# Attention block with gated MLP on one core: the last head set fed to the out-projection in padded layout, own MLP buffers for the last two chunks, and head loads on one queue

## The chip, the cores and the metric

The kernel runs on one core of a Trainium2 chip, as one launch. The metric is the device time in microseconds (us), the median over several executions. Lower is better. One further execution was recorded by the hardware profiler; all readings of single instructions, waits and stretches come from that record, which spans 899.9 us.

## The reference, cut to what matters

S = 2048 rows, D = 640, 32 heads of 20 columns, F = 1536, all bf16. The condition vector `c` gives six modulation vectors of 640 (shift, scale and gate for each half).

```python
mod = (silu(c) @ w_mod).reshape(1, 6, 1, 640)
sa, ca, ga, sb, cb, gb = mod[:, 0], ..., mod[:, 5]

h = layernorm(x) * (1 + ca) + sa
q, k, v = split_heads(h @ wqkv)                 # 32 heads of 20
p = softmax(q @ k.T * 20 ** -0.5)               # 32 x 2048 x 2048 scores
x = x + ga * (merge_heads(p @ v) @ wo)

h = layernorm(x) * (1 + cb) + sb
x = x + gb * (((h @ w_gate) * (h @ w_up)) @ w_down)
```

## The kernel before

The Python of the kernel does not emit its instructions in the order in which it is written. It builds tasks with dependencies, priorities and estimated durations, runs a small list scheduler over them at build time, and emits for each engine the order that came out, with semaphore waits in between. On the chip that order is fixed. Constants such as `QUADS`, `FILL_MIN` or `DMA_RATE` therefore change the order of instructions, or how many of a kind there are; nothing of them is read at run time.

The work is cut in five query chunks, and each chunk in eight head sets of four heads. Heads stand at a pitch of 32 partitions, so that four heads use the four row groups (scores) or the four column groups (attention times V) of TensorE at once.

```python
CHUNKS = [(0, 512), (512, 512), (1024, 512), (1536, 256), (1792, 256)]   # (first row, rows)
QUADS = [2, (2, 3, 3, 3, 3, 3, 3, 3), (2, 3, 3, 3, 3, 3, 3, 3), 1, 1]    # per chunk, or per head set
NPS = 8
D_RES = 8
FILL_MIN = 3400.0
LATEQ = ()
```

One unit of scores is 128 keys x 512 (or two times 128 keys x 256) of one head: one PSUM bank. Most units are turned to exponentials by ScalarE (ACT), three and two units in turn per instruction (groups of banks A and B). A "quad" is four units that VectorE (DVE) handles instead: it forms a 16-bit integer whose bits, read as bf16, approximate the exponential, and adds five shifted copies of it, all of which are multiplied with V:

```python
        def fexp(e, nu=nu, b0=b0, cellp=cellp):                       # ACT, 3 or 2 units
            return e.activation(PP[:, cellp["p"], 0:nu * 512],
                                ps[:, b0:b0 + nu, :].rearrange("p b c -> p (b c)"), AFT.Exp, scale=ESCALE)
...
            def fp1(e, st_=st_, x=x, cell=cell):                      # DVE, 4 per quad
                return e.tensor_scalar(DB0[:, st_["slot"], x * 512:(x + 1) * 512], bank(cell["b"]), EBIAS, 0.0,
                                       op0=ALU.add, op1=ALU.max)
...
            def fsh(e, st_=st_, cell=cell, jj=jj):                    # DVE, 5 per quad
                return e.tensor_scalar(DSS[:, cell["s"], :], DB0[:, st_["slot"], :], float(SHIFTS[jj]), None, op0=ALU.add)
```

The first loads go out on two queues, in this order of code (the last string but one is the issuing engine, the number its priority):

```python
    d_c = dma("act", 1280, ...)
    load_x(0, 0, "sp", 0);      load_x(0, 1, "act", 0.5)       # rows 0-255, 256-511
    load_wm(0, wm_a[0], "sp", 1);  load_wm(1, wm_a[1], "act", 1)   # modulation: shift, scale
    load_w(d_wk, 0, ..., "sp", 2); load_w(d_wq, 0, ..., "act", 2)  # half of Wk, of Wq
    load_x(1, 0, "sp", 1.5);    load_x(1, 1, "act", 1.5)
    ...
```

In chunk 0 the kernel also normalizes all rows, transposes them and projects K, V and Q; Q of the row blocks 1 to 3 stands at the end of that list. When a head set is done, DVE transposes the sum, divides by the softmax denominator (row 0 of each head's 32) and transposes back into `OcT`. There the heads lie at a pitch of 32 partitions; small DMAs move their 20 rows each into `Ocp`, where all 640 rows are dense in five blocks of 128:

```python
        t4 = dve(n * 1.1 + 65, lambda e: e.transpose(OcT[:, cell["s"], 0:n], OTn[:, 0:n]), [t3], prio=1.5)
        pcs = oc_pieces(j)                       # 4 or 5 pieces per head set
        ...
                return e.dma_start(Ocp[r0:r0 + nr, slot, b5, 0:n],
                                   OcT[32 * s + 1 + ro:32 * s + 1 + ro + nr, cell["s"], 0:n])
```

When the chunk's eight sets are in `Ocp`, `suffix(ci)` runs for it: out-projection, residual, second layernorm, gate and up projections, product, down-projection, store. For all but the last chunk these rounds are spread among the next chunk's attention, by gates that count exponential groups. All chunks share one set of buffers (`hprod`, `h2T`, `xck`, `xn2`):

```python
        d_xc = dma("sp", ..., lambda e: e.dma_start(xck[:, 0:ntl, :], xv[:, t0:t0 + ntl, :]),
                   out_prev + proj_early, prio=15, gate=max(0, gb - 20))    # residual rows
        for tl in range(ntl):
            for hf in range(2):
                for k in range(KD):                                          # KD = 5
                    f = quarters(320, lambda k=k, tl=tl: Ocp[:, slot, k, tl * 128:(tl + 1) * 128],
                                 lambda k=k, hf=hf: wo_sb[:, k, 320 * hf:320 * hf + 320], k == 0, k == KD - 1)
                ...
                r = Round(mms, list(oc_ready[ci]) + t_wo + [d_xc], after, pr(), gate=gate(KD * 320), name=f"op{ci}.{tl}")
```

`out_prev` are the stores of the chunk before, `proj_early` all projections. The gates `ga` and `gb` are multiplied into `wo` and `wd` (the down-projection weights) once, by GpSimd (POOL), after those weights are loaded; `wd` is loaded when the last projection has run, as its place was theirs. TensorE's idle time is filled with matmuls on the identity when the recent activity falls under `FILL_MIN`, to keep its clock up.

Of the kernel before, what the change touches and what calls it, by code (L numbers as in the profile page):

```python
# [18 lines left out]
DMA_RATE_2 = 180.0  # L19
DMA_SHARED = 12000.0  # L20
HAM_W = 3413.3
# [72 lines left out]
class Sched:  # L94
# [67 lines left out]
    def finish_issue(self, task, start, dur):  # L162
        task.start = start
        if task.nbytes:
            b = max(self.dma_free.get(task.eng, 0.0), start + dur)
            self.dma_free[task.eng] = b + task.nbytes / (DMA_RATE_2 if b < DMA_SHARED else DMA_RATE)
            task.done = self.dma_free[task.eng] + 1400.0
# [187 lines left out]
QUADS = [2, (2, 3, 3, 3, 3, 3, 3, 3), (2, 3, 3, 3, 3, 3, 3, 3), 1, 1]  # L355
# [3 lines left out]
NPS = 8  # L359
D_LATE = 12  # L360
D_RES = 8
PVMIN, PVMAX, PVCAP = 10, 10, 16
GATE_F = [0.7, 0.7, 0.6, 0.5, 1.0]
FILL_MIN = 3400.0
# [3 lines left out]
LN2P = 0.7  # L368
HT_L = 0.12
# [4 lines left out]
LATEQ = ()  # L374
LATEQ_A = 2
# [13 lines left out]
def build_kernel(nc, A_x, A_wqkv, A_wo, B_x, B_w_gate, B_w_up, B_w_down, c, w_mod, out):  # L389
# [97 lines left out]

    PP = alloc("PP", [128, NPS, 3 * 512], BF16)

# [43 lines left out]
    NSX = 11  # L533
    q_dead = sum(NSET * n * 2 for (_, n) in CHUNKS[:-1])
    nsx = min(NSX, q_dead // (2 * KD * 128 * 2))
    stx = [at("stx", [128, 2, KD, 128], BF16, qt_off + i * 2 * KD * 128 * 2) for i in range(nsx)]
# [5 lines left out]
    pP = Slots(list(range(NPS)), "PP")  # L542
# [29 lines left out]
    d_c = dma("act", 1280, lambda e: e.dma_start(c5[:, :], cv[:, :]), prio=0, dur=550.0)  # L572
# [19 lines left out]
    load_x(0, 0, "sp", 0)  # L592
    load_x(0, 1, "act", 0.5)
    load_wm(0, wm_a[0], "sp", 1)
    load_wm(1, wm_a[1], "act", 1)
    load_w(d_wk, 0, 1, wk_sb, 0, "sp", 2)
    load_w(d_wq, 0, 0, wq_sb, 0, "act", 2)
    load_x(1, 0, "sp", 1.5)
    load_x(1, 1, "act", 1.5)
# [157 lines left out]
    proj_early = []  # L757

# [4 lines left out]
    def kq_round(kind, j, tc, prio, gate=0):  # L763
# [33 lines left out]
        if kind == "K" or tc not in LATEQ:  # L797
            proj_early.append(r.last)

    def v_round(t, ch, prio, gate=0):  # L800
# [19 lines left out]
        proj_early.append(r.last)  # L820
# [128 lines left out]
    d_wo = dma("sp", 128 * KD * D * 2, lambda e: e.dma_start(wo_sb[:], wov[:, :, :]), prio=10)  # L949
    t_wo = []  # L950
    for k in range(KD):
        t_wo.append(pool(1400, lambda e, k=k: e.tensor_tensor(wo_sb[:, k, :], wo_sb[:, k, :], gab[:, 0, :], ALU.mult),
                         [d_wo] + ev_ga, prio=20))
# [30 lines left out]
    for g, (us, b0) in enumerate(glist):  # L984
# [14 lines left out]
        def fexp(e, nu=nu, b0=b0, cellp=cellp):  # L999
            return e.activation(PP[:, cellp["p"], 0:nu * 512],  # L1000
                                ps[:, b0:b0 + nu, :].rearrange("p b c -> p (b c)"), AFT.Exp, scale=ESCALE)
        if nu:
            ta = Task("act", nu * 512 / 1.2 + 52.0, fexp, [ts], prio=g, name=f"E{g}")
            ta.acq = [(pP, "p", nu)]

            def on_e(task, g=g, us=us, bset=bset, cellp=cellp):
# [3 lines left out]
                for i, u in enumerate(us):  # L1010
                    u.pslot = (pP, PP, task.slots["p"])
# [68 lines left out]

    oc_ready = {}
    oc_free = {}

    def item_end_tasks(it):
# [14 lines left out]
        pcs = oc_pieces(j)  # L1099
        t4.acq = [(sOcT, "s", len(pcs))]  # L1100
# [6 lines left out]
        for (b5, s, r0, nr, ro) in pcs:  # L1107
# [3 lines left out]
            dps = [t4]  # L1111
# [7 lines left out]
        oc_ready.setdefault(ci, []).extend(dms)  # L1119
        sc.left += 1  # L1120
# [3 lines left out]
    sfx_done = {}  # L1124
    sStg = [Slots(list(range(NSTG)), "stg") for _ in range(2)]
    out_prev = []

    def suffix(ci):
        nonlocal out_prev
# [17 lines left out]
        def pr():  # L1147
            return pbase + rc_[0]
# [519 lines left out]
```

The softmax here doesn't subtract the row's maximum and nothing guards it: scores larger than these inputs give would overflow.

## Time and profile before

| what | value |
|---|---|
| median of 3 executions | 897.82 us (897.0 to 901.93) |
| profiled execution | 899.9 us, mean granted TensorE clock 0.977 |
| exponentials on ACT | 695 instructions, 793.8 us, first at 23.2 us, last ends at 856.7 us |
| quads: first step, shifted copies (DVE) | 312 x 681 ns, 390 x 695 ns |
| copies into `Ocp` | 180 DMAs |

How to read it: a share of busy time is an average over the whole span. The stages differ: a head in which loads and projections come first, the long middle with its exponentials, and a tail that only the last chunk's MLP fills. So the views that follow are cut by stage. In a group's line stand the source line, the engine, the operation, what it writes and reads, how often it ran; then its busy time, the mean of one in ns, and the idle time of the engine before it with what ended it.

### The profile page before, as it was taken

What the parts mean: (1) busy time and instruction counts of PE and PEld (TensorE: products, weight loads), DVE (VectorE), ACT (ScalarE), POOL (GpSimd) and SP (SyncE); (2) the same over time, 40 slices, a digit from 0 to 9 for tenths busy, and PEclk for the clock granted to TensorE, in tenths of its full rate; (3) what the DMA queues carried; (4) which work ended last, traced back from release to release, by engine and by line L of the source; (5) the groups of instructions that cost most, each with busy time, mean ns of one, the idle gap of its engine ahead of it and who ended that gap; (6) DMA issues with size and microseconds to landing.
All of it is one profiled execution on the core that took longest, in us unless ns stands there. A gap on an engine that the chain in (4) does not pass through costs nothing.

```text
span 899.9 us, 31137 instructions
## 1 busy us (share of the span) xinstructions
PE 851.7 (95%) x13944; PEld 338.3 (38%) x13944; DVE 727.2 (81%) x1330; ACT 801.4 (89%) x712; POOL 56.8 (6%) x89
## 2 busy tenths in 40 slices
PE   6899999999999899999998999999999999999968
PEld 3434333333322222223333333333344445545547
DVE  6978677777868999899878999998888777688743
ACT  1567999999999789999999999999999999999901
POOL 4203000000000710000001000000010000000000
PEclk7989999999999889999999999999999999999999
DMA  9320000000006002210220011100301326405210
GB/s 307 103 75 7 5 6 5 2 6 6 5 5 166 2 20 50 50 34 6 49 64 5 23 44 42 42 6 20 74 27 28 70 65 129 95 28 109 51 32 18
DMA packets 100550, 42.31 MB, mean 47 GB/s; under 512 B 81218, under 2 KB 100418, under 8 KB 100418
## 3 DMA queue, kind: packets, MB, share of 16 engines
q1 hardware_dynamic: 98552, 38.44, 17.1%
q8 instruction: 110, 1.80, 0.8%
q10 hardware_dynamic: 1866, 1.89, 0.7%
q14 instruction: 22, 0.18, 0.1%
HBM read 35.06 MB, written 2.62 MB: 42 GB/s over the span
## 4 chain that ended last, share of the span: by engine, by line
PE 49%; ACT 32%; DVE 12%; issue 4%; POOL 1%; DMA 1%; SPq 0%; ACTq 0%; POOLq 0%; DVEq 0%
ACT PP L1000 32%; PE ps_all L653 15%; PE ps_all L969 14%; PE ps_all L1362 13%; PE ps_all L768 5%; DVE DSS L1038 2%; DVE DB L1024 2%; DVE xn L1180 1%; DMA x<-in_A_x_dram 1%; DVE st L711 1%; DVE st L1173 1%; DVE xck L1164 1%; POOL rs L1178 1%; DVE hT L746 1%; DVE xn L720 0%
## 5 line engine op out<-in xcount | busy, mean ns | idle before, releaser
L1000 ACT ACTIVATE PP<-ps_all 128x1536 bf16<-128x1536 f32 (+1 forms) x695 | 793.8, 1278 | 46.1 <-PE ps_all L969 42.3
L969 PE MATMUL ps_all<-QT,KT 32*128 32x512 bf16 (+1 forms) x2623 | 292.3, 343 | 14.5 <-ACT PP L1000 8.8
L1038 DVE TENSOR_SCALAR DSS<-DB 128x2048 int16<-128x2048 int16 x390 | 264.8, 695 | 29.5 <-PE ps_all L1362 27.1
L1024 DVE TENSOR_SCALAR DB<-ps_all 128x512 int16<-128x512 f32 x312 | 211.4, 681 | 42.8 <-PE ps_all L969 41.4
L969 PEld LDWEIGHTS ps_all<-QT,KT 32*128 32x128 bf16 x2623 | 76.4, 92 | 253.8 <-ACT PP L1000 175.6
L1362 PE MATMUL ps_all<-PP,Vf 128*32 128x512 bf16 (+3 forms) x2184 | 163.7, 343 | 0.7 <-DVE OT L1090 0.5
L1362 PE MATMUL ps_all<-DSS,Vf 128*32 128x512 bf16 (+2 forms) x1880 | 145.1, 349 | 0.5 <-DVE DSS L1038 0.2
L653 PE MATMUL ps_all<-h2T,stg 128*32 128x512 bf16 (+1 forms) x1960 | 130.6, 355 | 1.4 <-DVE DB L1024 0.9
L1362 PEld LDWEIGHTS ps_all<-PP,Vf 128*32 128x32 bf16 (+1 forms) x2184 | 50.9, 95 | 69.5 <-issue 57.7
L653 PE MATMUL ps_all<-wd,hprod 128*32 128x320 bf16 x1536 | 71.6, 301 | 0.7 <-DVE hprod L1245 0.5
L1362 PEld LDWEIGHTS ps_all<-DSS,Vf 128*32 128x32 bf16 (+1 forms) x1880 | 54.1, 97 | 27.3 <-DVE DSS L1038 4.7
L653 PEld LDWEIGHTS ps_all<-h2T,stg 128*32 128x32 bf16 x1960 | 41.7, 95 | 52.9 <-issue 26.0
L1176 POOL TENSOR_SCALAR sd<-mv 128x1 f32<-128x1 f32 x16 | 4.7, 293 | 747.0 <-DVE mv L1175 747.0
L768 PE MATMUL ps_all<-hT,wk 128*32 128x512 bf16 x640 | 48.0, 395 | 0.5 <-DVE gab L910 0.4
L768 PE MATMUL ps_all<-hT,wq 128*32 128x512 bf16 x640 | 46.3, 385 | 1.9 <-DVE DB L1024 1.3
L1245 DVE TENSOR_TENSOR hprod<-ps_all,gsb 128x512 bf16<-128x512 f32 (+1 forms) x60 | 34.6, 576 | 16.6 <-PE ps_all L653 16.3
L653 PEld LDWEIGHTS ps_all<-wd,hprod 128*32 128x32 bf16 x1536 | 35.9, 96 | 27.8 <-issue 16.4
L653 PE MATMUL ps_all<-wo,Ocp 128*32 128x320 bf16 x640 | 32.3, 310 | 7.8 <-DMA xck<-in_A_x_dram 3.4
L1235 DVE CAST gsb<-ps_all 128x512 bf16<-128x512 f32 (+1 forms) x48 | 29.6, 616 | 8.8 <-PE ps_all L653 8.6
L1090 DVE STREAM_TRANSPOSE OT<-ps_all 128x512 f32<-128x512 f32 (+1 forms) x40 | 24.2, 605 | 14.2 <-PE ps_all L1362 14.0
L1362 PE MATMUL ps_all<-DB,Vf 128*32 128x512 bf16 (+2 forms) x376 | 35.0, 349 | 0.0
L781 DVE TENSOR_SCALAR QT<-ps_all,qcol 128x512 bf16<-128x512 f32 (+1 forms) x40 | 24.9, 638 | 11.0 <-PE ps_all L768 10.8
(66 smaller groups left out, 451.7 us busy)
## 6 DMA issues: line engine op xcount, KB each, us to landing
stg<-in_B_w_gate_dram SPq DMA_DIRECT2D x49, 160.0 KB
stg<-in_B_w_up_dram SPq DMA_DIRECT2D x49, 160.0 KB
out_dram<-xck SPq DMA_DIRECT2D x16, 160.0 KB
wm<-in_w_mod_dram SPq DMA_DIRECT2D x3, 800.0 KB
x<-in_A_x_dram SPq DMA_DIRECT2D x6, 320.0 KB
xck<-in_A_x_dram SPq DMA_DIRECT2D x3, 640.0 KB
wd<-in_B_w_down_dram SPq DMA_DIRECT2D x1, 1920.0 KB
stx<-in_B_w_gate_dram SPq DMA_DIRECT2D x11, 160.0 KB
```

The costliest lines, as they stand in the source:

```text
L653: return lambda e, b: e.matmul(ps[32 * x:32 * x + 32, b, 0:n], lhs()[:, 32 * x:32 * x + 32], rhs(), tile_position=(0, 32 * x), start=st, s ...
L711: bns.append(dve(393, lambda e, t=t, i=i, hf=hf: e.bn_stats(st[:, i, 6 * hf:6 * hf + 6], x0[:, t, 320 * hf:320 * hf + 320]), [d_x[tc][i // ...
L768: f = [lambda e, b, k=k, s=s: e.matmul(ps[32 * s:32 * s + 32, b, :], wx[:, k, w0 + DH * s:w0 + DH * s + 32], hT[tc][:, k, :], tile_positio ...
L781: f = lambda e, ci=ci, so=so, n=n: e.tensor_scalar(QT[ci][:, j, :], ps[:, r.b["b"], so:so + n], qcol[:, 0:1], None, op0=ALU.mult)
L969: ems.append(lambda e, i=i, kt=kt: e.matmul(dstf()[:, i * u.n:(i + 1) * u.n], KT[32 * u.s:32 * u.s + 32, u.j, kt * 128:(kt + 1) * 128], QT ...
L1000: return e.activation(PP[:, cellp["p"], 0:nu * 512], ps[:, b0:b0 + nu, :].rearrange("p b c -> p (b c)"), AFT.Exp, scale=ESCALE)
L1024: return e.tensor_scalar(DB0[:, st_["slot"], x * 512:(x + 1) * 512], bank(cell["b"]), EBIAS, 0.0, op0=ALU.add, op1=ALU.max)
L1038: return e.tensor_scalar(DSS[:, cell["s"], :], DB0[:, st_["slot"], :], float(SHIFTS[jj]), None, op0=ALU.add)
L1090: t1 = Task("dve", n * 1.1 + 70, lambda e: e.transpose(OT[:, 0:n], ps[:, BPV, 0:n]), [], prio=0.0, name=f"T1.{it}")
L1235: f = lambda e: e.tensor_copy(gsb[:, gs, 0:n], ps[:, r.b["b"], 0:n])
L1245: f = lambda e: e.tensor_tensor(hprod[:, fc, 0:n], ps[:, r.b["b"], 0:n], gsb[:, gs, 0:n], ALU.mult)
L1362: ems.append(lambda e, i=i, kt=kt, stt=stt, stp=stp: e.matmul(ps[32 * s:32 * s + mc, BPV, 0:u.n], Vf[:, (kt * H + 4 * u.j + s) * VW:(kt * ...
```

## The change

Several parts belong together.

- The last head set of each chunk (heads 28 to 31) is no longer copied into `Ocp`. The out-projection reads it from `OcT`, with a weight block `wo7` whose rows stand at the same pitch of 32 and are zero between the heads. The out-projection so has six contraction blocks, the fifth partly zero. This takes four DMAs per chunk away.
- The MLP of the last two chunks gets own buffers (`set_t` where Q of chunks 0 and 1 lay, `set_c` in the region of the shared set), so that they need not wait for the chunk before. Other dependencies are made finer (`kv_last`, `v_last`).
- The head's loads all go to the SP queue, in the order of need.
- Q of the row blocks 2 and 3 is projected in chunk 1 (`LATEQ`).
- The ring of exponentials is split in one for groups of three and one for groups of two, which frees the room for `wo7`.
- Constants of the build-time order: more quads, none of the two free PSUM banks held back for quads (`D_RES`), a higher filler threshold, another estimate of DMA rates.

```diff
-DMA_RATE_2 = 180.0
+DMA_RATE_2 = 330.0
+DMA_LAT = 1700.0
...
-QUADS = [2, (2, 3, 3, 3, 3, 3, 3, 3), (2, 3, 3, 3, 3, 3, 3, 3), 1, 1]
+QUADS = [(1, 2, 2, 3, 2, 3, 2, 3), 3, 3, 1, 1]
-NPS = 8
+NPS = 4
-D_RES = 8
+D_RES = 100
-FILL_MIN = 3400.0
+FILL_MIN = 4200.0
+NALT = 1
-LATEQ = ()
-LATEQ_A = 2
+LATEQ = (2, 3)
+LATEQ_A = 0
...
-    PP = alloc("PP", [128, NPS, 3 * 512], BF16)
+    PPs = [alloc("PP", [128, NPS, w * 512], BF16) for w in (3, 2)]
+    wo7 = alloc("wo7", [128, D], BF16)
...
+        set_t = (T.alloc("hprodt", [128, FT, ntail], BF16), T.alloc("h2Tt", [128, KD, ntail], BF16),
+                 T.alloc("xckt", [128, ntail // 128, D], BF16), T.alloc("xn2t", [128, ntail // 128, D], BF16))
...
-    load_x(0, 0, "sp", 0)
-    load_x(0, 1, "act", 0.5)
+    load_x(0, 0, "sp", 0.1)
+    load_x(0, 1, "sp", 0.2)
     load_wm(0, wm_a[0], "sp", 1)
-    load_wm(1, wm_a[1], "act", 1)
+    load_wm(1, wm_a[1], "sp", 1.1)
+    load_x(1, 0, "sp", 1.5)
+    load_x(1, 1, "sp", 1.6)
     load_w(d_wk, 0, 1, wk_sb, 0, "sp", 2)
-    load_w(d_wq, 0, 0, wq_sb, 0, "act", 2)
-    load_x(1, 0, "sp", 1.5)
-    load_x(1, 1, "act", 1.5)
+    load_w(d_wq, 0, 0, wq_sb, 0, "sp", 2.1)
...
+z_wo = pool(400, lambda e: e.memset(wo_sb[:, KD - 1, :], 0.0), prio=8)
+z_w7 = pool(400, lambda e: e.memset(wo7[:], 0.0), prio=8)
...
+    t_wo.append(pool(1400, lambda e: e.tensor_tensor(wo7[:], wo7[:], gab[:, 0, :], ALU.mult), d_w7 + ev_ga, prio=20))
...
-        pcs = oc_pieces(j)
+        pcs = oc_pieces(j) if j < NSET - 1 else []
...
+        bd = bset_done[1 if NALT and ci == NC - 2 else 0]
+        hprod, h2T, xck, xn2 = set_r if not alt else set_t if ci == NC - 2 else set_c
...
-                   out_prev + proj_early, prio=15, gate=max(0, gb - 20))
+                   (first if alt else bd.get("out", []) + v_last), prio=15, gate=max(0, gb - 20))
...
-                                 lambda k=k, hf=hf: wo_sb[:, k, 320 * hf:320 * hf + 320], k == 0, k == KD - 1)
+                                 lambda k=k, hf=hf: wo_sb[:, k, 320 * hf:320 * hf + 320], k == 0, False)
                     mms.append((C320, f))
+                f = quarters(320, lambda tl=tl: OcT[:, oc_last[ci]["s"], tl * 128:(tl + 1) * 128],
+                             lambda hf=hf: wo7[:, 320 * hf:320 * hf + 320], False, True)
+                mms.append((C320, f))
```

## The prediction

> **What bounds the kernel now.** I first read the page: shares of busy time, the slices, the granted clock.
>
> ```profile
> PE 851.7 (95%) x13944; PEld 338.3 (38%) x13944; DVE 727.2 (81%) x1330; ACT 801.4 (89%) x712; POOL 56.8 (6%) x89
> ...
> ACT  1567999999999789999999999999999999999901
> PEclk7989999999999889999999999999999999999999
> ```
>
> PE's 95% overstates it: a matmul's modelled end overlaps the next one's start. ACT is full outside three places: the first four slices, slices 13 and 14, the last two. To see what each stage lacks I cut the span at the transposes that end a head set: 73 us ends the first set, 253, 461, 653 and 758 end query chunks 0 to 3, and 858 is chunk 4's last one. The view is the busy time of each engine in given stretches (columns: stretch, length, busy us of PE, weight load, DVE, ACT and POOL with counts, clock, DMA share, GB/s).
>
> ```profile
> 0.00:23.00 23.00, 15.04 (x149) 6.91 (x149) 15.24 (x53) 3.14 (x5) 9.43 (x24) 0.78 1.00 309
> 23.00:73.00 50.00, 46.88 (x699) 20.05 (x696) 43.01 (x95) 32.27 (x29) 6.34 (x16) 0.93 0.23 76
> 73.00:99.00 26.00, 24.84 (x408) 10.03 (x407) 19.76 (x33) 21.42 (x20) 8.10 (x5) 1.00 0.03 7
> 99.00:253.00 154.00, 151.86 (x2162) 49.84 (x2162) 115.65 (x191) 153.54 (x136) 0.00 (x0) 1.00 0.02 5
> 279.00:344.00 65.00, 57.27 (x685) 17.69 (x687) 59.54 (x100) 53.95 (x48) 22.40 (x20) 0.87 0.26 67
> 461.00:653.00 192.00, 185.73 (x2593) 61.78 (x2591) 175.00 (x301) 189.51 (x168) 3.48 (x8) 0.99 0.15 36
> 758.00:858.00 100.00, 97.60 (x2379) 54.75 (x2371) 73.31 (x150) 98.56 (x88) 1.94 (x4) 1.00 0.35 79
> 858.00:900.00 42.00, 31.19 (x838) 23.87 (x829) 15.20 (x38) 4.46 (x12) 1.58 (x4) 0.96 0.08 23
> ```
>
> So the exponentials on ACT set the pace from 99 to 253 us and in chunks 2 to 4. ACT stands 17.7 us in the first head set, 4.6 in the second, 11.1 between 279 and 344. Before 23 us it has nothing to do, and after 858 us it is done. The gain must come from these holes or from fewer exponentials. In the first set the waits name the lack of scores (to column: us, times, longest):
>
> ```profile
> ACT PP L1000 <- PE ps_all L969: 23.0, 5, 7.4
> ```
>
> The tail, in order of time (start, length, what):
>
> ```profile
> 859.01 0.43 DVE L1098 STREAM_TRANSPOSE OcT<-OTn 128x256 bf16<-128x256 bf16 x1
> 859.47 1.48 SPq L1109 DMA_DIRECT2D Ocp<-OcT  x2
> ...
> 861.52 1.49 SPq L1109 DMA_DIRECT2D Ocp<-OcT  x2
> 863.11 0.42 SPq L1149 DMA_DIRECT2D xck<-in_A_x_dram  x1
> 866.02 2.90 PE L653 MATMUL ps_all<-wo,Ocp 128*32 128x320 bf16 x80 [3.45 <-DMA xck<-in_A_x_dram]
> ```
>
> The last attention output is ready at 859.44. Four small copies, then the load of the residual rows, which waited for the previous chunk's last store (issued at 860.99), hold the out-projection until 866.02.
>
> The two holes in mid-kernel coincide with multiplications on POOL (groups of 82 to 320 us, and DVE's own group of 293 to 318 us):
>
> ```profile
> L957 POOL TENSOR_TENSOR wd<-wd,gab 128x640 bf16<-128x640 bf16 x12 | 18.0, 1519 | 0.2 <-DMA wd<-in_B_w_down_dram 0.2
> L952 POOL TENSOR_TENSOR wo<-wo,gab 128x640 bf16<-128x640 bf16 x5 | 8.1, 1650 | 39.7 <-DVE gab L910 39.7
> ...
> L1038 DVE TENSOR_SCALAR DSS<-DB 128x2048 int16<-128x2048 int16 x9 | 8.9, 992 | 0.0
> ```
>
> The shifted copies take 992 ns there, 695 over the whole run.
>
> **What the Trainium skill says.** "SBUF — State Buffer", section "SBUF: two separate sides": VectorE and GpSimd share one port pair as an exclusive lock. The 992 against 695 ns agrees; the change keeps these multiplications and adds one. "DMA: Bandwidth & Descriptors", section "Issuing engines are not separate DMA queues": loads from two issuers share the same 16 engines and interleave. It agrees: from 20 to 30 us only the SP queue issues, and 314 GB/s flow; from 10 to 20 us it is 330. So one queue costs no rate, and the order decides who lands first. "TensorE: Matmul & The Clock Gate", section "Part 1: The HAM clock gate": an idle window of about 3.4 us halves the clock. The trace shows half-clock stretches of 3.4 or 6.8 us: 48.2 to 55.0, 307.7 to 314.5, 321.3 to 328.1, and 874.3 to 877.7.
>
> **The change part by part.**
>
> *Head loads.* Before, the second half of the first rows landed at 7.8 us, the second modulation block at 11.6, the first query weights at 16.0, because both queues interleaved. In need order, the rows (2 x 320 KB) and the two blocks (2 x 800 KB) are 2.29 MB; at 278 GB/s, the rate of the first 10 us, 8.3 us. Two more row halves and two weight halves make 3.77 MB: 10 + (3.77 - 2.78)/0.33 = 13.0 us. Both stand 3 us earlier, and normalization, transposes and the first K and Q follow them. First exponential 23.2 -> about 20.2: **-3.0**.
>
> *Fewer exponentials.* Quads (four 512-wide units by bit tricks on DVE instead of ACT) go from 16, 23, 23, 8, 8 to 18, 24, 24, 8, 8: four more, 16 units. ACT spends 793.8 us on 1736 units, 0.457 each: -7.3 us, of which chunk 0 has 8 units (-3.7), chunks 1 and 2 four each (-1.8). DVE pays 4 x 0.68 + 5 x 0.695 = 6.2 us a quad. From 99 to 253 us it has 38 us free, so there the **-3.7** is real.
>
> *First head set.* It has one quad instead of two: 6.2 us less on DVE, which is 86% busy there with normalization, V and K. Of the 17.7 us of ACT idle I take **-4.5**.
>
> *Q of row blocks 2 and 3.* Sixteen rounds (20 matmuls each; one that ran unbroken, at 236.19 us, took 1.26 us of PE) move from the end of chunk 0 into the first 35% of chunk 1. In chunk 0 ACT was full anyway, so nothing falls there. In chunk 1 the MLP of chunk 0 no longer waits for the last Q at 277 us. But DVE was busy 20.3 + 59.5 + 106.1 = 186 us of chunk 1's 208; one quad (+6.2) and the evacuations not there before (about +4.4) make 197 against 190 for ACT. At 96% busy that is 205: **-3**. The wd multiplication waits for the last Q and moves later, into a fuller DVE.
>
> *Chunk 2.* -1.8 of ACT, DVE 175 + 6.2 = 181 in some 190: **-2** with a little of its 2.5 us idle.
>
> *Chunks 3 and 4.* The same exponentials. Own buffers let chunk 3's MLP start at its gate, not at 789 us when chunk 2's stores are out. That was beside full ACT: **0** here, but its down-projection, which ran until about 860, leaves the tail.
>
> *Tail.* No copies, and the residual rows are there: out-projection at about 859.5 instead of 866.0, -6.5. A sixth contraction block adds 16 matmuls x 36 ns (2.90 us / 80) = 0.6, of which 0.5 reaches the end. The half-clock stretch at 874.3 costs 1.6 (the first two gate rounds end after 1.31 and 1.96 us, later ones are 1.09 apart); half of that may go, as less idle lies ahead and the filler threshold rises: -0.8. Sum **-6.8**. In the other chunks the 16 removed copies (20 in all) and the extra 112 matmuls lie beside ACT.
>
> *Fillers and bank reserve.* A higher activity threshold and no bank held back for quads: some of the half-clock time at 48 and 308 to 328 us may go, **-2**. Splitting the exponential ring in 3-wide and 2-wide halves gives the same alternating run-ahead: 0.
>
> Sum: -3.0 - 3.7 - 4.5 - 3 - 2 - 0 - 6.8 - 2 = -25.0; 897.8 - 25 = 872.8.
>
> **The rivals.** (a) *Chunk 1 turns DVE- and PE-bound.* For it: 197 us of DVE, 16 Q rounds (16 x 1.26 = 20 us of PE) beside the out-projection and gate work in the same third, and POOL's lock. Against it: three-quad sets ran at 22 to 23 us in late chunk 1. Then chunk 1 takes 215 to 220 and the total is about 884. (b) *The head is bound by DVE, not by loads*: DVE is busy 43 of 50 us, so an earlier start is paid back by 73 us; the -3 and half of the -4.5 vanish: 878. (c) *Holes close further than I count*: with the Q rounds out of the way all of ACT's 11 us in chunk 1 and most of the first set's idle go: 860. (d) *The tail copies were hidden by chunk 3's down-projection* until 860.1: only if that stays late; then the tail gives 5.9, not 6.5.
>
> **Range and chances.** Solid are the tail and chunk 0's exponentials (-10.5); the rest (-14.5) depends on an order set at build time by an estimate of durations. (a) and (c) span 860 to 884, a little wider: 858 to 887. 2% faster is 879.9; the estimate lies 7 us under it with a spread of some 11: 0.70 faster, 0.26 within, 0.04 slower.
>
> **What would show it.** Right: first exponential near 20 us; ACT idle in the first set near 13; 688 exponentials, 328 and 410 quad instructions; chunk 1 near 205 with DVE over 95% busy; the out-projection of the last chunk within 0.3 us of the last transpose, with 96 matmuls; some 36 us from last exponential to end. Wrong: a new wait of ACT on scores in early chunk 1 beyond 15 us, or a first exponential at 23 us, or chunk 3's down-projection still in the tail.

## The result and the profile after

| | before | after |
|---|---|---|
| median of 4 executions | 897.41 us (895.89 to 901.93) | 887.99 us (887.0 to 891.07) |
| profiled execution | 899.9 us, clock 0.977 | 886.4 us, clock 0.990 |

The ratio is 0.9893, 95% interval 0.985 to 0.9936: a gain of 9.4 us, about 1%, where 25 were predicted. The time lies 1 us above the range.

The page of the changed kernel, its busy shares and slices:

```profile
PE 846.1 (95%) x14095; PEld 341.1 (38%) x14095; DVE 749.9 (85%) x1366; ACT 797.1 (90%) x705; POOL 62.2 (7%) x94
...
ACT  1688999999999978999999999999999999999911
PEclk7999999999999998999999999999999999999999
```

Of the three dents in ACT's line, the first is smaller, the second has moved one slice to the right, the third is still two slices long. The same span cut at the transposes that end head sets (65 us ends the first, 242, 446, 640, 745 and 846 the five chunks; 318 to 354 is the fourth set of chunk 1; columns as in the prediction):

```profile
22.00:65.00 43.00, 40.63 (x664) 17.64 (x668) 36.04 (x85) 31.95 (x28) 8.92 (x20) 1.00 0.34 105
...
93.00:242.00 149.00, 146.24 (x2084) 47.63 (x2072) 126.23 (x212) 147.64 (x131) 0.00 (x0) 1.00 0.07 16
...
318.00:354.00 36.00, 29.15 (x351) 9.30 (x347) 35.11 (x55) 27.36 (x23) 20.91 (x18) 0.91 0.04 8
...
446.00:640.00 194.00, 187.25 (x2659) 64.30 (x2648) 177.15 (x309) 189.50 (x166) 3.90 (x8) 1.00 0.14 33
...
846.00:887.00 41.00, 35.08 (x1122) 29.91 (x1114) 19.45 (x49) 4.47 (x12) 1.58 (x4) 1.00 0.21 52
```

Two lines matter most. In the fourth set of chunk 1 DVE is busy 35.1 of 36 us and ACT stands 8.6; the sets around it last 21.7 to 26.2 us. In the tail PE has 1122 matmuls, where the tail of before had 838: work has come into it. ACT's waits for scores in the first set (columns: us, times, longest) were 23.0 us before and are shorter:

```profile
ACT PP L1035 <- PE ps_all L1004: 16.8, 4, 6.3
```

The length of each stage, in us, against the prediction. A stage ends here with the first transpose of a set's sum:

| stage | before | after | change | predicted |
|---|---|---|---|---|
| start to first exponential | 23.2 | 22.5 | -0.7 | -3.0 |
| first head set | 49.7 | 42.5 | -7.2 | -4.5 |
| rest of chunk 0 | 180.1 | 176.7 | -3.4 | -3.7 |
| chunk 1 | 207.6 | 204.1 | -3.5 | -3 |
| chunk 2 | 192.1 | 194.1 | +2.0 | -2 |
| chunks 3 and 4 | 205.3 | 206.5 | +1.2 | 0 |
| tail | 42.0 | 40.0 | -2.0 | -6.8 |
| fillers and reserve, in no stage | | | | -2 |
| sum | 900.0 | 886.4 | -13.6 | -25.0 |

The execution of before that was profiled was itself one of the longer ones. A second profile of the kernel before (903.5 us; run e_before2) spreads as 23.0, 47.8, 181.6, 211.1, 190.7, 205.3 and 44.0 us, so a stage is uncertain by 2 us, chunk 1 by 3.5, and what is only 2 us in this table carries no argument alone.

### The profile page after: what moved, and what is told of

Same layout as the page of the kernel before. It is cut to its first block, busy times and chain, and to the rows that moved or that the text cites. A ratio compares the mean times of both kernels' runs of the same rounds, so it can differ in the third digit from the quotient of the medians.

```text
span 886.4 us, 31394 instructions
## 1 busy us (share of the span) xinstructions
PE 846.1 (95%) x14095; PEld 341.1 (38%) x14095; DVE 749.9 (85%) x1366; ACT 797.1 (90%) x705; POOL 62.2 (7%) x94
## 4 chain that ended last, share of the span: by engine, by line
PE 63%; DVE 18%; ACT 13%; issue 2%; DMA 2%; POOL 1%; SPq 0%; DVEq 0%; ACTq 0%
PE ps_all L677 22%; PE ps_all L1004 18%; PE ps_all L1415 17%; ACT PP L1035 13%; PE ps_all L794 6%; DVE DSS L1073 5%; DVE DB L1059 4%; DMA wm<-in_w_mod_dram 1%; DVE QT L807 1%; DVE st L1223 1%; DVE xn L1230 1%; DVE hT L770 1%; POOL rs L1228 1%; DVE xck L1213 1%; PE ps_all L1241 1%
## 5 line engine op out<-in xcount | busy, mean ns | idle before, releaser
L1035 ACT ACTIVATE PP<-ps_all 128x1536 bf16<-128x1536 f32 (+1 forms) x688 | 789.3, 1256 | 39.7 <-PE ps_all L1004 36.7
L1073 DVE TENSOR_SCALAR DSS<-DB 128x2048 int16<-128x2048 int16 x410 | 283.2, 707 | 29.1 <-PE ps_all L1415 27.0
L1059 DVE TENSOR_SCALAR DB<-ps_all 128x512 int16<-128x512 f32 x328 | 222.6, 683 | 39.2 <-PE ps_all L1004 37.6
L1415 PE MATMUL ps_all<-PP,Vf 128*32 128x512 bf16 (+2 forms) x2168 | 161.8, 341 | 0.2 <-DVE OT L1128 0.2
L1415 PE MATMUL ps_all<-DSS,Vf 128*32 128x512 bf16 (+3 forms) x1960 | 147.9, 346 | 2.4 <-DVE DSS L1073 2.2
L677 PE MATMUL ps_all<-h2T,stg 128*32 128x512 bf16 x1440 | 110.1, 383 | 2.1 <-DVE DB L1059 1.5
L677 PE MATMUL ps_all<-wd,hprod 128*32 128x320 bf16 x1152 | 54.9, 302 | 0.0
L677 PEld LDWEIGHTS ps_all<-h2T,stg 128*32 128x32 bf16 x1440 | 30.0, 95 | 52.4 <-issue 27.7
L677 PEld LDWEIGHTS ps_all<-wd,hprod 128*32 128x32 bf16 x1152 | 26.0, 96 | 19.6 <-issue 13.5
L677 PE MATMUL ps_all<-wV,hT 128*32 128x320 bf16 x640 | 30.9, 302 | 0.7 <-DVE DB L1059 0.5
L803 DVE CAST KT<-ps_all 128x512 bf16<-128x512 f32 x32 | 22.0, 687 | 8.7 <-PE ps_all L794 8.7
```

The lines of the kernel that those rows point to most:

```text
L677: return lambda e, b: e.matmul(ps[32 * x:32 * x + 32, b, 0:n], lhs()[:, 32 * x:32 * x + 32], rhs(), tile_position=(0, 32 * x), start=st, s ...
L803: f = lambda e: e.tensor_copy(KT[:, j, tc * 512:(tc + 1) * 512], bank(r.b["b"]))
L1035: return e.activation(PPs[g % 2][:, cellp["p"], 0:nu * 512], ps[:, b0:b0 + nu, :].rearrange("p b c -> p (b c)"), AFT.Exp, scale=ESCALE)
L1415: ems.append(lambda e, i=i, kt=kt, stt=stt, stp=stp: e.matmul(ps[32 * s:32 * s + mc, BPV, 0:u.n], Vf[:, (kt * H + 4 * u.j + s) * VW:(kt * ...
```

## The experiments

**e_before2** is the kernel before, once more, as a measure of how far two of its profiles differ; its stages stand above.

> The kernel before once more, for a second profile of it: stages within 2 us of the first profile (49.7, 180.1, 207.6, 192.1, 104.5, 100.8, tail 42), except where a half-clock stretch fell differently; the first profile's 899.9 us lay some 4 us over the median, so up to 4 us less in chunk 1.

Each of the other kernels is the changed one with the edit shown. Times are medians, the ratio is to the kernel before, with its 95% interval; "after" is 887.99 us, 0.9893. The median of the kernel before moved between 897.4 and 898.9 us from one set of runs to the next, so 1 or 2 us between two rows show nothing. The table gives the stages and, as "backlog", the matmuls of chunk 3's MLP still to run when the last exponential ends. e_wd16 and e_split4 keep the order of after, and e_bestsplit that of e_best; most other edits also make another order of instructions, and such a row shows the part together with its order.

| run | us | ratio | first exp | set 1 | rest of chunk 0 | chunk 1 | chunk 2 | chunks 3, 4 | tail | backlog |
|---|---|---|---|---|---|---|---|---|---|---|
| before | 897.41 | 1 | 23.2 | 49.7 | 180.1 | 207.6 | 192.1 | 205.3 | 42.0 | 80 |
| after | 887.99 | 0.9893 | 22.5 | 42.5 | 176.7 | 204.1 | 194.1 | 206.5 | 40.0 | 352 |
| e_copy | 892.96 | 0.9937 [0.9919, 0.9955] | 22.4 | 42.5 | 176.7 | 204.1 | 195.9 | 203.0 | 46.4 | 460 |
| e_shared | 909.33 | 1.0123 [1.0098, 1.0147] | 21.6 | 42.5 | 176.7 | 204.8 | 194.1 | 206.6 | 61.0 | 552 |
| e_nodn3 | 887.60 | 0.9887 [0.9857, 0.9918] | 22.2 | 42.5 | 176.7 | 203.6 | 194.1 | 206.8 | 38.0 | 176 |
| e_nomlp3 | 887.17 | 0.9866 [0.9828, 0.9903] | 22.0 | 42.5 | 176.7 | 204.0 | 194.1 | 207.4 | 38.1 | 0 |
| e_heads2 | 893.84 | 0.9956 [0.994, 0.9971] | 23.4 | 45.1 | 177.0 | 208.2 | 189.8 | 206.3 | 41.0 | 352 |
| e_quads0 | 894.24 | 0.9944 [0.9924, 0.9965] | 22.2 | 45.4 | 181.2 | 206.2 | 192.0 | 204.8 | 40.3 | 192 |
| e_quads12 | 897.22 | 0.999 [0.9972, 1.0007] | 22.7 | 42.5 | 176.7 | 204.8 | 195.5 | 212.4 | 41.8 | 272 |
| e_lateq0 | 888.77 | 0.9886 [0.9851, 0.9921] | 22.5 | 42.5 | 177.3 | 203.2 | 189.5 | 211.8 | 39.3 | 260 |
| e_fillres | 892.34 | 0.9942 [0.9921, 0.9964] | 21.5 | 44.5 | 177.1 | 205.2 | 190.7 | 205.8 | 45.1 | 472 |
| e_wd16 | 880.40 | 0.9803 [0.978, 0.9826] | 23.2 | 42.5 | 176.7 | 195.3 | 194.1 | 206.6 | 40.6 | 352 |
| e_split4 | 890.78 | 0.9919 [0.9899, 0.994] | 23.0 | 42.5 | 175.1 | 208.1 | 194.1 | 207.1 | 40.1 | 352 |
| e_spread | 892.11 | 0.9948 [0.9931, 0.9966] | 22.6 | 42.6 | 178.1 | 203.1 | 198.7 | 201.0 | 43.4 | 492 |
| e_best | 881.63 | 0.9826 [0.9808, 0.9843] | 22.8 | 42.5 | 178.1 | 200.5 | 194.0 | 204.9 | 37.5 | 100 |
| e_bestsplit | 877.69 | 0.9768 [0.9738, 0.9799] | 22.9 | 42.6 | 178.1 | 196.7 | 193.9 | 205.0 | 37.1 | 100 |

### The tail: was the copies' wait real, and what took its place?

My theory after the result: the wait was real and is gone, but chunk 3's MLP, which now runs in buffers of its own and is still unfinished, fills the gap. The rival: the copies had been hidden all along (rival d in full).

Before, the wait was real. The last matmul of chunk 3's down-projection ended at 860.09 us; then came 11 fillers, and 3.45 us of nothing until the out-projection at 866.02:

```profile
860.02 2.55 PE L1595 MATMUL ps_all<-ident 128*128 128x512 bf16 x11
```

The tail of the changed kernel, in order of time (start, length, what):

```profile
847.90 0.44 DVE L1136 STREAM_TRANSPOSE OcT<-OTn 128x256 bf16<-128x256 bf16 x1
...
848.39 0.86 PE L677 MATMUL ps_all<-wo,Ocp 128*32 128x320 bf16 x20
...
850.76 1.28 PE L677 MATMUL ps_all<-h2Tt,stg 128*32 128x256 bf16 x37
...
853.48 6.82 PE L677 MATMUL ps_all<-wd,hprodt 128*32 128x320 bf16 x192
...
856.56 0.45 DVE L1230 TENSOR_SCALAR xn2c<-xckc,mv,rs 128x640 bf16<-128x640 bf16 x1 [0.62 <-POOL rs L1228]
...
860.23 0.73 PE L1241 MATMUL ps_all<-ident,xn2c 128*128 128x128 bf16 x10
```

The out-projection starts 0.05 us after the last output transpose ends at 848.34; before, it was 6.6. But between its rounds PE works through chunk 3's last gate and up rounds, and then runs chunk 3's whole down-projection (192 matmuls, 6.82 us). The last chunk's normalized rows are ready at 857.01 and stand until 860.23. From the last output transpose to the transposes of the normalized rows it is 11.9 us; before, 13.3. In all of that stretch PE is never idle (columns as above):

```profile
848.34:860.23 11.89, 11.89 (x357) 9.31 (x349) 7.96 (x20) 0.00 (x0) 1.58 (x4) 1.00 0.39 90
```

Of what starts in it, 96 matmuls are the out-projection, 60 gate and up of chunk 3, and 192 its down-projection.

**e_copy**: the copies come back, by a new order of the build; nothing else in the source changes.

```diff
-        pcs = oc_pieces(j) if j < NSET - 1 else []
+        pcs = oc_pieces(j)                        # and no sixth contraction block, no wo7
```

> The changed kernel, but the last head set is copied into the dense layout by DMA again, and the out-projection has five contraction blocks. Backlog theory (what chunk 3's MLP has left fills TensorE in the tail anyway): the copies delay the out-projection by about 3.5 us after the last transpose, but the 6.8 us of chunk 3's down-projection fit in there, so the total is 0 to 2 us longer than the changed kernel's 888.0. Direct theory of the prediction (the wait for the copies is a loss of its own): 4 to 6.5 us longer.

It is 5.0 us slower than after, and its tail is 6.4 us longer. From its timeline:

```profile
847.60 3.00 SPq L1139 DMA_DIRECT2D Ocp<-OcT  x4
...
851.75 1.54 PE L677 MATMUL ps_all<-wo,Ocp 128*32 128x320 bf16 x40 [0.27 <-DMA Ocp<-OcT]
...
857.89 6.70 PE L677 MATMUL ps_all<-wd,hprodt 128*32 128x320 bf16 x192 [0.50 <-DVE hprodt L1281]
...
864.53 0.73 PE L1226 MATMUL ps_all<-ident,xn2c 128*128 128x128 bf16 x10
```

Its last output transpose ends at 846.44; the out-projection follows 5.3 us later, the transposes of the rows 18.1 us later, against 11.9. But PE does not stand while the copies run:

```profile
846.45:851.75 5.30, 4.10 (x122) 2.94 (x123) 2.66 (x7) 0.00 (x0) 0.00 (x0) 1.00 0.51 114
```

It works on chunk 3's gate and up rounds, of which the new order has more left: 200 such matmuls start between the last output transpose and the transposes of the rows, 60 in after. At 1.26 us for 40 of them, the 140 more are an estimated 4.4 of the 6.2 us. So e_copy does not isolate the copies. It fits the direct theory by its total, but for the most part through the backlog; what the copies alone cost beside this backlog stays open, and for the changed kernel rival (d) is not refuted.

**e_shared**: the last two chunks share the common buffers again (`NALT = 1` becomes `0`, and one assignment moves out of its branch).

> The changed kernel with one set of MLP buffers for all chunks (own buffers undone). Backlog theory: chunk 3's MLP starts about 40 exponential groups later, after chunk 2's stores, and most of it falls in the tail: 10 to 22 us longer than the changed kernel. If own buffers only shift work that lies beside the exponentials anyway: 0 to 4 us longer.

21 us slower than after, all in the tail (61.0 us, 552 matmuls of chunk 3 left). Of the 672 matmuls of chunk 3's MLP own buffers bring 200 more to their end before the last exponential. They were more necessary than the prediction had them, which gave them 0: with shared buffers the kernel before had 80 left, so it is the other parts of the change that push MLP work later.

**e_nodn3** leaves out 11 of the 12 contraction blocks of chunk 3's down-projection, 176 of 192 matmuls. **e_nomlp3** leaves out the same and 11 of 12 of its gate and up blocks.

```diff
-                for fc in range(FT):                                   # down-projection, e_nodn3 and e_nomlp3
+                for fc in range(1 if ci == NC - 2 else FT):
-        for fc in range(FT):                                           # gate and up, e_nomlp3 alone
+        for fc in range(1 if ci == NC - 2 else FT):
```

> The changed kernel with 11 of the 12 contraction blocks of chunk 3's down-projection left out (192 matmuls become 16; that work is not done). Backlog theory: these 6.2 us stand between the second layernorm and the last chunk's transposes in the tail; 3 to 5 us shorter than the changed kernel, and the transposes of the last chunk come 8.7 us after the last output transpose instead of 11.9. If the tail is the last chunk's own chain and this work is hidden in its gaps: 0 to 1 us shorter.

> The changed kernel with 11 of 12 blocks of chunk 3's gate, up and down projections left out (440 + 176 matmuls; that work is not done). Backlog theory: all that chunk 3 has left at the last exponential (352 matmuls in the changed kernel) goes, the last chunk runs its own chain alone; the stretch from the last output transpose to the end falls from 40.0 to about 35.5 us and the total by 4 to 6 us. Rival (the 2 us that leaving out the down-projection took from that stretch are all there is): 1 to 2.5 us shorter.

Neither gave the gain that its missing work suggests: -0.4 and -0.8 us of the median, -2.0 and -1.9 of the tail. In e_nodn3 the rows are transposed 10.2 us after the last output transpose instead of 11.9. DVE's order is fixed, and the four residual adds of chunk 3 (853.74 to 855.41) now stand in front of the last chunk's own add. In e_nomlp3 it is 7.1 us, so the chain of the last chunk alone is that short. But then PE, busy 5.0 of 7 us, falls to half clock. Busy time of each engine in stretches of e_nomlp3 (the last but two column is the clock):

```profile
848.00:855.00 7.00, 4.99 (x103) 2.99 (x103) 4.68 (x12) 0.00 (x0) 1.58 (x4) 1.00 0.01 2
855.00:862.00 7.00, 6.06 (x106) 4.67 (x110) 2.42 (x7) 0.74 (x2) 0.00 (x0) 0.51 0.01 2
```

Half clock from 855.1 to 861.9: from the rows' transposes to the end it takes 29.8 us, against 26.2 in after. So the backlog does delay the last chunk, by 11.9 - 7.1 = 4.8 us, which is most of the 6.5 that the removed wait should have brought, but most of what taking the work out gains is lost again at half clock. e_lateq0, e_quads0, e_quads12, e_best and e_bestsplit, with backlogs of 100 to 272, have a half-clock stretch of 3.4 us in the tail as well (e_nodn3, with 176, has none before its last 1.1 us).

### Chunk 1: what makes the fourth set 36 us long?

The view is the groups of 317 to 340 us of the changed kernel (busy, mean ns):

```profile
L992 POOL TENSOR_TENSOR wd<-wd,gab 128x640 bf16<-128x640 bf16 x12 | 18.6, 1563 | 3.4 <-DMA wd<-in_B_w_down_dram 3.4
L1073 DVE TENSOR_SCALAR DSS<-DB 128x2048 int16<-128x2048 int16 x8 | 10.0, 1262 | 0.0
```

The shifted copies take 1262 ns beside POOL's multiplications; elsewhere (93 to 242 us) they take 682.

**e_wd16** multiplies only 16 of the 640 columns of each `wd` block, in the same order on all engines. It so leaves most of the gate out of the down-projection's weights.

```diff
-        ... e.tensor_tensor(wd_sb[:, f_, :], wd_sb[:, f_, :], gab[:, 1, :], ALU.mult)
+        ... e.tensor_tensor(wd_sb[:, f_, 0:16], wd_sb[:, f_, 0:16], gab[:, 1, 0:16], ALU.mult)
```

> The changed kernel in the very same order on all engines, but POOL's twelve multiplications of the down-projection weights take 16 of 640 columns each (the rest is not multiplied, so the gate is left out of most of the output). Lock theory (POOL's multiplications hold VectorE back, scores come late, TensorE's clock falls): ACT's idle 8.3 us in the fourth head set of chunk 1 goes, chunk 1 falls from 204 to 195-198 us, total 5 to 9 us shorter. Rival (that head set is long because VectorE and TensorE have Q, layernorm and quads to do there): chunk 1 within 2 us of 204, total within 2 us.

7.6 us faster than after. That set takes 27.3 us instead of 36.0, every other head set agrees within 0.2 us, and the first exponential and the tail cost 0.7 and 0.6 us more. Its groups of 309 to 341 us:

```profile
L1073 DVE TENSOR_SCALAR DSS<-DB 128x2048 int16<-128x2048 int16 x17 | 11.5, 683 | 0.0
...
L992 POOL TENSOR_TENSOR wd<-wd,gab 128x16 bf16<-128x16 bf16 x12 | 3.6, 320 | 2.4 <-DMA wd<-in_B_w_down_dram 2.4
```

The whole set, to be held against the line of 318 to 354 us of after:

```profile
318.27:345.54 27.27, 26.29 (x353) 9.32 (x351) 27.23 (x55) 26.58 (x24) 4.99 (x15) 1.00 0.05 11
```

The hole is POOL's burst. Twelve multiplications cost the set 8.7 us. DVE's busy time for the same operations falls from 35.1 to 27.2, so 7.9 of the 8.7 us are longer operations of DVE: shifted copies (974 ns on average in that set, 683 in e_wd16), normalizations (1106, 436) and one division (1867, 674). That DVE's layernorm waits for its power step on POOL, behind the burst, would be the other way to the same hole; in that set of after DVE has no such wait. The half-clock stretches of chunk 1 (330.3 and 343.9, 3.4 us each) are gone with them, so they belong to it.

**e_split4** cuts each multiplication of `wo` and `wd` in four pieces of 160 columns, in the same order.

```diff
-    e.tensor_tensor(wd_sb[:, f_, :], wd_sb[:, f_, :], gab[:, 1, :], ALU.mult)
+    for cs in PCS: e.tensor_tensor(wd_sb[:, f_, cs], wd_sb[:, f_, cs], gab[:, 1, cs], ALU.mult)
```

> The changed kernel in the same order, but each of POOL's multiplications of out-projection and down-projection weights is cut in four pieces of 160 columns. Lock theory: VectorE waits for a piece of about 0.4 us at most, not for 1.5; the shifted copies in that stretch fall from 1262 to under 900 ns on average, chunk 1 by 2 to 6 us, the second head set by 0 to 2, total 2 to 7 us shorter. Rival: POOL's fixed cost per instruction makes the stretch longer, total 0 to 3 us longer.

Slower than after by 2.8 us in the median, though the times overlap (887.4 to 892.3 against 887.0 to 891.1 us). The sets show more. The set with the `wo` multiplications got shorter (28.2 to 26.6 us), the one with `wd` longer (36.0 to 40.0), though DVE's copies were quicker: POOL now took 26.0 us for the 12 blocks (48 x 576 ns) instead of 18.6, and DVE stood 10.3 us of that set, 0.9 in after. Chunk 0's second layernorm has its power step on POOL, among the burst in POOL's order, and here DVE does wait for it (columns: us, times, longest):

```profile
DVE xn L1232 <- POOL rs L1230: 6.5, 3, 2.7
```

**e_spread** moves each multiplication between rounds that come anyway: `wd` block fc after chunk 0's gate round fc, `wo` block k after the V projection of a row block.

```diff
-        ... ALU.mult), [d_wd] + ev_gb, prio=21))
+        ... ALU.mult), [d_wd, eg] + ev_gb, prio=21))       # eg: evacuation of gate round fc
```

> The changed kernel with POOL's multiplications spread: each of the twelve for the down-projection waits for one gate evacuation of chunk 0's MLP, each of the six for the out-projection for one V evacuation in chunk 0. All work is done. Lock theory (it is the burst, over VectorE's layernorm and quads, that costs 8.7 us): no head set of chunk 1 over 28 us, ACT idle there under 2 us, chunk 1 near 196; the build's other order in the tail takes up to 4.5 back: 879 to 885 us. Rival (each multiplication holds VectorE wherever it stands): chunk 1 over 202, total 887 to 892.

The fourth set falls to 27.3 us as hoped, but three of the four that follow are 2.2 to 3.7 us longer, chunk 1 gains only 1.0, and the new order has the largest backlog but one (492): 4.1 us slower in all. A whole multiplication seems to cost DVE its share wherever it stands, but the new order alone could make these sets longer too; e_bestsplit below tests the remedy.

### The other parts, one at a time

**e_heads2** gives the head loads back to two queues in the old order of code.

> The changed kernel with the first loads on two queues again, in the old order. Prediction's step (one queue in need order lands the first blocks 3 us earlier): first exponential 3 us later, near 25.5 us, total 3 us longer. Rival (landings lag the flow, and the head is paced by VectorE and the half-clock TensorE): first exponential within 1 us of 22.5, total within 2 us, apart from what the other build-time order does.

First exponential +0.9, first set +2.6, in all 5.8 us slower. One queue with its order is the better choice, but it acts less through the first exponential than through the first set. What held the first exponential, from the timeline of after:

```profile
2.78 1.98 DVE L711 TENSOR_SCALAR ex<-ex 128x5 f32<-128x5 f32 x1 [0.27 <-ACT ex L710]
...
9.98 0.83 PE L691 MATMUL ps_all<-scol,wm 128*128 128x1 bf16 x25 [3.79 <-DMA wm<-in_w_mod_dram]
...
12.24 0.74 PEld L691 LDWEIGHTS ps_all<-scol,wm 128*128 128x128 bf16 x25 [1.03 <-DMA wm<-in_w_mod_dram]
```

The second modulation block is waited for until 12.24 us; before, until 11.62. The prediction had it at 8.3. By 2 us stretches, 2.45 MB had flowed by 10 us (1, 225, 324, 323 and 353 GB/s) and 2.29 by about 9.5: the flow starts later than before and is slower (2.78 MB by 10 us before). If the loads flow strictly in their order, which was not tried, the block is usable 2.7 us after its last byte has passed. The flow from 6 to 8 us in after, then in e_heads2 with its two queues (last column GB/s):

```profile
6.00:8.00 2.00, 0.19 (x1) 0.00 (x0) 2.00 (x8) 0.00 (x0) 0.50 (x2) 1.00 0.97 323
6.00:8.00 2.00, 0.00 (x0) 0.00 (x0) 0.69 (x3) 0.00 (x0) 0.31 (x1) 1.00 1.07 373
```

From 4 to 6 us it is 324 and 381. So in the first 10 us the prediction's "one queue costs no rate" does not hold; it had compared stretches after 10 us.

The first line of the timeline is a side matter: 5 elements per partition take 1.98 us on DVE and end as POOL's memset of 2.37 to 4.73 us ends, so that DVE's first statistics stand at 5.95 instead of 3.77. They were not what came last.

**e_quads0** has the quads of before. **e_quads12** has them in chunks 1 and 2 only.

```diff
-QUADS = [(1, 2, 2, 3, 2, 3, 2, 3), 3, 3, 1, 1]
+QUADS = [2, (2, 3, 3, 3, 3, 3, 3, 3), (2, 3, 3, 3, 3, 3, 3, 3), 1, 1]                             # e_quads0
+QUADS = [(1, 2, 2, 3, 2, 3, 2, 3), (2, 3, 3, 3, 3, 3, 3, 3), (2, 3, 3, 3, 3, 3, 3, 3), 1, 1]     # e_quads12
```

> The changed kernel with the quads of the kernel before (78 instead of 82; first head set two instead of one). If ScalarE sets the pace as the prediction had it: 7.3 us more exponentials and a slower first head set, 9 to 12 us longer. If VectorE and TensorE set the pace of chunks 1 and 2: those two stay within 2 us of 204 and 194, only chunk 0 grows by 5 to 8, total 4 to 8 us longer.

> The changed kernel with the one extra quad in chunk 1 and in chunk 2 undone (chunk 0's quads stay changed). If ScalarE set the pace there, as the prediction's terms for chunks 1 and 2 had it: 3.6 us longer, near 891.6. If VectorE and TensorE do: chunks 1 and 2 together within 2 us of 398, total within 2 us of 888 apart from the tail, for which the build's own order gives up to 3 us more.

e_quads0 is 6.2 us slower; chunk 0 alone loses 7.4 (first set 2.9, the rest 4.5). From there to the end it is 1.4 us faster than after (643.3 against 644.7): in chunks 1 and 2 the extra quads, in this order, bring nothing. e_quads12 was to show that by itself and missed. Chunks 1 and 2 took 400.3 us, after 398.2, but the new order put a half-clock stretch (812.9 to 819.7 us) into chunk 4 and held its out-projection 5.8 us behind the last transpose. The total says more of this than of the quads.

**e_lateq0** puts Q of row blocks 2 and 3 back on the list of chunk 0 (`LATEQ = ()`). **e_fillres** has the old filler threshold and bank reserve (`FILL_MIN = 3400`, `D_RES = 8`).

> The changed kernel with all of Q projected at the end of chunk 0 again (LATEQ empty). If the move of Q into chunk 1 is what delays chunk 0's MLP, and so all later ones down to the tail: MLP of chunk 0 is done 10 exponential groups sooner, fewer than 352 matmuls of chunk 3 are left at the last exponential, total 1 to 4 us shorter, chunk 0 as long as now. If the move gave chunk 0 its 11 us: chunk 0 3 to 6 us longer, total 0 to 3 us longer.

> The changed kernel with the filler threshold and the bank reserve of the kernel before (3400 and 8). Prediction's step (-2 for both): 2 us longer. Rival (they only reorder): within 1 us, or longer by what the other order costs in the tail, up to 4 us as the build's own estimate has it.

e_lateq0 makes no difference to the total: 4.6 us in chunk 2 come back as 5.3 in chunks 3 and 4. But it hardly moves Q: of its 640 matmuls 280 still run in chunk 1, where after has 304 and before had 144. So what the late Q is worth was not tested. e_fillres is 4.3 us slower: 2.0 in the first set, 5.1 in the tail with a backlog of 472, 3.4 less in chunk 2. Its rows are transposed no later than in after (11.1 us); there the backlog lies behind them, with 32.5 us to the end against 26.2.

### A kernel faster than both

**e_best** takes the spread multiplications, the old quads in chunks 1 and 2, priority for the out-projection's rounds and a wider window for the late Q. **e_bestsplit** is the same with each `wd` multiplication in four pieces, in the same order.

```diff
-OPFIRST = 0
+OPFIRST = 600
-LATEQ_F = 0.35
+LATEQ_F = 0.5
-    e.tensor_tensor(wd_sb[:, fc, :], wd_sb[:, fc, :], gab[:, 1, :], ALU.mult)       # e_bestsplit alone
+    for cs in PCS: e.tensor_tensor(wd_sb[:, fc, cs], wd_sb[:, fc, cs], gab[:, 1, cs], ALU.mult)
```

> As e_spread, and with the second and third chunk's quads of the kernel before (23 each; the first chunk keeps the changed kernel's 18), chunk 0's out-projection ahead of the late Q rounds, and these stretched over half of chunk 1. If the quads added in chunks 1 and 2 brought nothing, as undoing all of them let it seem, and the MLP comes in time: chunks 1 and 2 no longer than in e_spread, under 150 MLP matmuls of chunk 3 left at the last exponential, total 873 to 880 us. If ScalarE sets the pace there: 3.6 us longer than e_spread.

> The kernel of e_best in the same order, with each multiplication of the down-projection weights cut in four pieces of 160 columns. If VectorE's waits at whole multiplications cost about 0.65 us each in chunk 1 (203.1 in e_spread against 195.3 with 16 columns, over twelve): 2 to 5 us shorter than 881.6. Rival (pieces hold VectorE as long in sum): within 1 us.

881.63 and 877.69 us, the second 2.3% faster than before. e_best has a backlog of 100 and a tail of 37.5 us: this order leaves little of chunk 3's MLP for the end. The groups of 242 to 442 us of e_best, then of e_bestsplit:

```profile
L1072 DVE TENSOR_SCALAR DSS<-DB 128x2048 int16<-128x2048 int16 x115 | 81.5, 723 | 5.7 <-PE ps_all L1417 5.1
```

```profile
L1073 DVE TENSOR_SCALAR DSS<-DB 128x2048 int16<-128x2048 int16 x118 | 80.7, 697 | 5.9 <-PE ps_all L1419 5.1
...
L1295 POOL TENSOR_TENSOR wd<-wd,gab 128x160 bf16<-128x160 bf16 x48 | 30.2, 660 | 118.5 <-DMA wd<-in_B_w_down_dram 68.5 <-DVE gsb L1286 49.9
```

POOL is busy 30.2 us instead of 18.5, and still chunk 1 shrinks from 200.5 to 196.7: the longest shifted copy falls from 1889 to 974 ns. Spread as they are here, the pieces make DVE wait for POOL nowhere in chunk 1; in one burst (e_split4) they did.

## Why the prediction was wrong

Of the 25.0 us, chunk 0 came as predicted in sum: -11.2 predicted, -11.3 measured at its end. That is partly luck: the first exponential gave 0.7 instead of 3.0, the first set 7.2 instead of 4.5, and some 2 us of that belong to the fillers' term. From the start of chunk 1 to the end 13.8 were predicted and 2.3 came (647.0 to 644.7 us):

- **Tail: the failed step.** "its down-projection, which ran until about 860, leaves the tail" is false; it ran from 853.48 to 860.3, and the prediction had named that as a sign of being wrong. The out-projection's start behaved as worked out (6.6 to 0.05 us). The half-clock stretch is gone too: the first gate rounds end 1.09 us apart at once, and from the rows' transposes to the end it is 26.2 us instead of 27.2. But PE fills the freed time with chunk 3's work, and the backlog keeps the rows 4.8 us longer than e_nomlp3's chain needs, and the tail gave -2.0 instead of -6.8. Rival (d) had named this, with the condition "only if that stays late", and I priced it at 0.6 us; the price was the error. I checked when chunk 3's MLP may start, not when its work would be done.
- **Why it stayed late.** The step "Own buffers let chunk 3's MLP start at its gate" took an early start for an early end. The same happened in chunk 1. Chunk 0's out-projection does start sooner (258.4 us instead of 281.7), as the prediction had it, but chunk 1 of after contains 664 matmuls of out-projection and MLP, before 980; Q has 304 there instead of 144. Chunk 0's last store is out at 496.9 us, 51 us after chunk 1's end; before, 5 us. Chunk 2's last store comes at 809.0 instead of 787.5. The delay travels along to chunk 3's backlog of 352. The runs show that backlog and tail depend on the build-time order as a whole (e_lateq0 260, e_quads0 192, e_fillres 472, e_best 100). Which single part makes the 352 was not settled: `LATEQ = ()` takes 92 of them away, though it hardly moves Q, the quads 160.
- **Chunk 2 (-2, measured +2.0), chunks 3 and 4 (0, +1.2).** From the start of chunk 1 to the end it is 643.3 to 645.3 us in after, e_lateq0, e_quads0 and e_heads2, whose single stages differ by up to 7 us; e_quads12, with a half-clock stretch in chunk 4, has 654.5. What one chunk gains another gives back; I read this as work left at a chunk's end moving on, which the store times above fit but no run shows alone. Adding per-chunk savings up was wrong there.
- **Quads of chunks 1 and 2** (-1.8 each, inside the chunks' terms): not seen in e_quads0, where undoing them cost nothing. DVE was idle only 11.3 of chunk 1's 204.1 us. Nor did ACT gain the whole 7.3: its exponentials took 789.3 us after 793.8. The term of chunk 0 (-3.7) was about right, e_quads0 says 4.5 outside the first set.
- **Chunk 1** came out at 204.1 against 205 predicted, with DVE busy 94.5% of it. Rival (a), 215 to 220 us, did not come. Against the second profile of before it gains 7, against the first 3.5. The POOL burst was kept in the sum as unchanged, and was; e_wd16 says it is worth 8.7 us, more than any term of mine.
- **Head loads (-3.0): mis-sized, -0.7.** Bytes over rate gave 8.3 us for the second block; it was usable at 12.24. The missing part is a later and slower flow (1.2 us) and some 2.7 us between the flow and the landing. The first set gained 7.2 instead of 4.5. By e_heads2 2.6 of it comes from the loads, by e_quads0 2.9 from its quad, by e_fillres 2.0 from fillers and reserve. With the 0.9 at the first exponential the loads bring 3.5 by e_heads2: the size was about right, but most of it does not come through an earlier first exponential.
- **Fillers and reserve (-2): right in sign, too small.** e_fillres measures 4.3 in all, of which 2.0 lie in the first set and the rest in the tail and through the order; no stage of its own shows it. Half-clock time between 25 and 860 us fell from 27.2 us to 6.8, both stretches that are left being those of POOL's burst; what that brought cannot be told apart. (The prediction's list lacks the stretches of before at 10.7, 283.8 and 488.6 us; the first, 10.2 us long, is still there.)
- **The base.** I subtracted savings read in a 899.9 us profile from the median. Of the 13.6 us gained between the profiles, 9.4 show in the medians.

In sum, 25.0 - 9.4 = 15.6 us were missed: 4.8 in the tail, 4.0 in chunk 2, 1.2 in chunks 3 and 4, 2.0 in a term for fillers beside stages that already hold their gain, 4.2 in the base (13.6 - 9.4), less 0.6 that chunks 0 and 1 brought beyond the prediction.

## What to carry to other kernels

A wait taken off the last chain is worth its length only if the engine it frees has nothing else queued in front of that chain: before pricing it, count what unfinished work stands there and ask whether the change adds to it. In a kernel whose order is fixed at build time, per-stage savings don't add; compare from a common point to the end. And find what a hole costs by shrinking its suspected cause in place with the order unchanged, as e_wd16 does, before moving it.

## What the runs showed of the hardware that was not expected

- The Trainium skill, "SBUF — State Buffer", section "SBUF: two separate sides", has some VectorE operations and GpSimd exclude each other on a shared port pair. The traces agree and give the size for the shifted copies: 682 ns alone, 1262 beside back-to-back multiplications of 1.56 us each, and 8.7 us of a head set for twelve of them, two half-clock stretches of PE included. Not all of VectorE is slowed: the quads' first steps, which read PSUM, take 668 ns in that set and 675 in e_wd16, the transposes back into `OcT` 695 and 700.
- Cutting such a GpSimd instruction in four makes it dearer on GpSimd (1542 to 4 x 660 ns) and cheaper for VectorE (longest copy 1889 to 974 ns).
- With 616 matmuls of chunk 3 left out (e_nomlp3), the kernel ended less than 1 us earlier by the median: PE fell to half clock for 6.8 us of the tail.
- With all head loads on one queue 324 and 323 GB/s flowed from 4 to 6 and from 6 to 8 us (after), with two queues and the old order 381 and 373 (e_heads2).
